# A gated two-branch spectral filter on one core: symmetric folds, a real-packed spectrum and quarter-size transforms in place of transposes

## The chip, the cores and the metric

The kernel runs on one NeuronCore of one Trainium2 chip. The metric is the device time of one execution in microseconds (us). "PE" is the matmul engine and "PEld" its weight loads, "DVE" the vector engine, "ACT" the scalar engine; "SPq" is the queue of the SyncE engine, which here only issues DMAs. Every number comes from a run or from its profile.

The times of the kernel before scatter: of its 11 runs beside one group of experiments, four took 301.8 to 305.1 us and seven 306.9 to 312.1; the latter are marked slow (over 1.5% above the fastest). By the same rule one of the four runs in the table below, that of 310.48 us, is slow, and so is the profiled execution, by its span of 309.5 us (in the runs listed the span is about 1.8 us below the time).

Ratios here are those of the fast runs of the same rounds, so not quite the ratios of the medians that I quote. Differences of about 1% between groups of runs should not be read.

## The reference

```python
def branch(x, w_r, w_i):                       # x: (1, 2048, 1024) bf16, w: (2048, 513)
    X = rfft2(x.astype(float32))               # over both axes
    return irfft2(X * (w_r + 1j * w_i), s=(2048, 1024)).astype(bfloat16)

g = sigmoid((x * gate_w).sum(-1, keepdims=True))
out = g * branch(x, A_w_r, A_w_i) + (1 - g) * branch(x, B_w_r, B_w_i)
```

The forward transform of x is shared. Each branch (A and B) multiplies the spectrum by its own weights W_A or W_B (4.2 MB each) and transforms back. Both kernels do this as small dense transforms by matmul: d (1024 columns) in one factor, the 2048 rows as 128 x 16.

## The kernel before

Each stage is a loop on PE; ACT and DVE evict PSUM between them (they copy the results of the matmuls, `PS` in the views, to the tiles of the next stage). The parts that matter here:

```python
# x is transposed by matmuls with IDENT, then the d transform: 16 x 8 x 3 matmuls of 342 columns
for n2 in range(16):
    for j in range(8):
        lhsT = AP(R_XT, j * 2048 + n2 * 128, ...)
        for ch in range(3):
            mm = e.matmul(bank(bset + ch, 0, ncols), lhsT, rhs, start=(j == 0), stop=(j == 7))      # L218
# ... 64 + 64 matmuls (L234, L240) ...
for g in range(16):                                    # 512 small transposes, L258
    for tt in range(8):
        for lh in range(4):
            mm = e.matmul(AP(PS, (32 * lh) * PSRS + ...), lhsT, IDENT[:], tile_position=(0, 32 * lh))
# ... K-point transform (L289/L290), then per branch the products on DVE and L312/L313 on PE,
#     inverse over n1 (L336), inverse over d: 16 x 2 x 8 matmuls of 512 columns (L360)

# the loads of W, in pieces of 128 elements (256 bytes); B's start when the d transform is over
@block.sync
def _(e):
    ...
    e.wait_ge(sem("pe_j1"), 16)
    w_dmas(e, 1, R_XT, "d_wB", (0, 2))
```

Of the kernel before, what the change touches and what calls it, by code (L numbers as in the profile page):

```python
# [4 lines left out]
dt = mybir.dt  # L5
ACT = mybir.ActivationFunctionType
ALU = mybir.AluOpType
AP = bass.AP

S, D, L = 2048, 1024, 513  # L10
NCOLX = 2 * 16 * L
NX = 128 * 128


def bf16_bits(a):
    a = np.ascontiguousarray(np.asarray(a, dtype=np.float32))
    u = a.view(np.uint32).astype(np.uint64)
    r = ((u + 0x7FFF + ((u >> 16) & 1)) >> 16).astype(np.uint16)
    return r


def make_consts():
    C = {}
    dd = np.arange(128)[:, None, None]
    j = np.arange(8)[None, :, None]
    l = np.arange(L)[None, None, :]
    ang = 2 * np.pi * ((128 * j + dd) * l % D) / D
    DF = np.concatenate([np.cos(ang), -np.sin(ang)], axis=2)
    C["DF"] = DF[:, 0:4, :].reshape(128, 4 * 2 * L)
    sg = (-1.0) ** np.arange(L)  # L30
    C["SGN"] = np.broadcast_to(np.concatenate([sg, sg])[None, :], (128, 2 * L)).copy()
    n1 = np.arange(128)[:, None, None]
    n2 = np.arange(16)[None, :, None]
    k1 = np.arange(128)[None, None, :]
    ph = -2 * np.pi * ((n1 * k1 * 16 + n2 * k1) % 2048) / 2048.0
    U2 = np.zeros((128, 16, 3, 128))
    U2[:, :, 0, :] = np.cos(ph)
    U2[:, :, 1, :] = np.sin(ph)
    U2[:, :, 2, :] = -np.sin(ph)
    C["U2"] = U2.reshape(128, 16 * 3 * 128)  # L40
    C["IDENT"] = np.eye(128)
    C["ONES"] = np.ones((128, 128))
    a16 = np.arange(16)
    th = 2 * np.pi * np.outer(a16, a16) / 16
    M16 = np.zeros((32, 32))
    M16[0:16, 0:16] = np.cos(th); M16[16:32, 0:16] = np.sin(th)
    M16[0:16, 16:32] = -np.sin(th); M16[16:32, 16:32] = np.cos(th)
    M16i = np.zeros((32, 32))
    M16i[0:16, 0:16] = np.cos(th); M16i[16:32, 0:16] = -np.sin(th)
    M16i[0:16, 16:32] = np.sin(th); M16i[16:32, 16:32] = np.cos(th)  # L50
    M16s = np.concatenate([M16[:, 16:32], M16[:, 0:16]], axis=1)
    M16iA = np.concatenate([M16i[0:16, :], -M16i[0:16, :]], axis=0)
    M16iB = np.concatenate([M16i[16:32, :], M16i[16:32, :]], axis=0)
    KF2 = np.zeros((128, 128)); KF2S = np.zeros((128, 128))
    KIA = np.zeros((128, 128)); KIB = np.zeros((128, 128))
    for lh in range(4):
        KF2[lh * 32:(lh + 1) * 32, lh * 32:(lh + 1) * 32] = M16
        KF2S[lh * 32:(lh + 1) * 32, lh * 32:(lh + 1) * 32] = M16s
        for r in range(32):
            for cc in range(32):  # L60
                KIA[lh * 32 + r, cc * 4 + lh] = M16iA[r, cc]
                KIB[lh * 32 + r, cc * 4 + lh] = M16iB[r, cc]
    C["KF2"] = KF2; C["KF2S"] = KF2S; C["KIA"] = KIA; C["KIB"] = KIB
    def pad128(m):
        o = np.zeros((128, m.shape[1])); o[0:m.shape[0]] = m
        return o
    C["M16PK"] = np.concatenate([pad128(M16), pad128(M16s), pad128(M16iA), pad128(M16iB)], axis=1)
    k1b = np.arange(128)[:, None, None]
    o2 = np.arange(16)[None, :, None]
    o1 = np.arange(128)[None, None, :]  # L70
    ph5 = 2 * np.pi * ((k1b * o1 * 16 + o2 * k1b) % 2048) / 2048.0
    U5 = np.zeros((128, 16, 4, 128))
    U5[:, :, 0, :] = np.cos(ph5) / S
    U5[:, :, 1, :] = np.sin(ph5) / S
    U5[:, :, 2, :] = -np.sin(ph5) / S
    U5[:, :, 3, :] = np.cos(ph5) / S
    C["U5"] = U5.reshape(128, 16 * 4 * 128)
    ll = np.arange(128)[:, None]
    dcol = np.arange(D)[None, :]
    Dinv = np.zeros((128, 8, D))  # L80
    for lh in range(4):
        lval = 128 * lh + ll
        cl = np.where(lval == 0, 1.0, 2.0) / D
        ang3 = 2 * np.pi * ((lval * dcol) % D) / D
        Dinv[:, lh * 2 + 0, :] = cl * np.cos(ang3)
        Dinv[:, lh * 2 + 1, :] = -cl * np.sin(ang3)
    C["DINV"] = Dinv.reshape(128, 8 * D)
    C["NSPAT"] = np.broadcast_to((((-1.0) ** np.arange(512)) / D)[None, :], (128, 512)).copy()
    one = np.zeros((128, 2)); one[:, 0] = 1.0
    C["ONE"] = one  # L90
    return C


def bass_gated_mix__spectral_gfnet__spectral_gfnet__prompt_kernel(
# [3 lines left out]
    cst = {k: nc.inline_tensor(bf16_bits(v), name=f"c_{k}") for k, v in C.items()}  # L98

    bfz = dt.bfloat16  # L100
    sb = lambda name, shape, dty=dt.bfloat16: nc.alloc_sbuf_tensor(name, shape, dty)
    R_XT = sb("R_XT", [128, 8 * 2048])
    R_L1 = sb("R_L1", [128, NCOLX])
    R_L2 = sb("R_L2", [128, NCOLX])
    R_C1 = sb("R_C1", [128, NCOLX])
    R_W = sb("R_W", [128, NCOLX])
    R_L4A = sb("R_L4A", [128, NCOLX])
    SGN = AP(R_L4A, 4096, [[NCOLX, 128], [1, 2 * L]])
    IDENT = sb("IDENT", [128, 128]); ONES = sb("ONES", [128, 128])
    KF2 = sb("KF2", [128, 128]); KF2S = sb("KF2S", [128, 128]); KIA = sb("KIA", [128, 128]); KIB = sb("KIB", [128, 128])  # L110
    M16PK = sb("M16PK", [128, 4 * 32])
    GWT = sb("GWT", [128, 8]); ONE2 = sb("ONE2", [128, 2])
    NSPAT = sb("NSPAT", [128, 512]); GROW = sb("GROW", [128, 2048])
    RBUF = sb("RBUF", [128, 2, 2, 2, 256])
    L3S = sb("L3S", [128, 128])
    XST = sb("XST", [128, 2, 128])
    WST = sb("WST", [128, 2, 128])
    PST = sb("PST", [128, 2, 128])
    G = sb("G", [128, 16], dt.float32); ZT = sb("ZT", [128, 16], dt.float32)
    PS = nc.alloc_psum_tensor("PS", [128, 4096], dt.float32)  # L120

    with nc.Block() as block:
        sems = {}
        info = {"n_c": 11}

        def sem(name):
            if name not in sems:
                sems[name] = nc.alloc_semaphore(name)
            return sems[name]

        rsX = 8 * 2048
        rs = NCOLX
        PSRS = 4096

        def bank(b, c0=0, n=512, p0=0, np_=128):
            return AP(PS, p0 * PSRS + b * 512 + c0, [[PSRS, np_], [1, n]])

        x2 = A_x[0]
        out2 = out[0]
        wsrc = {0: (A_w_r, A_w_i), 1: (B_w_r, B_w_i)}  # L140
        BN = "AB"

        def w_dmas(e, bb, region, semname, lhs):
            for c in range(2):
                for lh in lhs:
                    src = wsrc[bb][c][:, 128 * lh:128 * lh + 128].rearrange("(k2 k1) ll -> k2 k1 ll", k1=128)
                    dst = region[lh * 32 + c * 16: lh * 32 + c * 16 + 16, 0:NX].rearrange("p (k1 ll) -> p k1 ll", ll=128)
                    e.dma_start(dst, src).then_inc(sem(semname), 16)

        def wstar_dmas(e, bb, semname):  # L150
            for c in range(2):
                src = wsrc[bb][c][:, 512:513].rearrange("(k2 k1) o -> k2 (k1 o)", k1=128)
                with nc.allow_non_contiguous_dma(reason="N* W column gather (small)"):
                    e.dma_start(WST[c * 16:(c + 1) * 16, bb, :], src).then_inc(sem(semname), 16)

        @block.sync
        def _(e):
            e.dma_start(IDENT[:].bitcast(dt.uint16), cst["IDENT"].ap()).then_inc(sem("d_id"), 16)
            xv = x2.rearrange("(p r) d -> p r d", r=16)
            for h in range(2):  # L160
                e.dma_start(AP(R_L2, 8192 * h, [[rs, 128], [1024, 8], [1, 1024]]), xv[:, 8 * h:8 * h + 8, :]).then_inc(sem(f"d_x{h}"), 16)
            e.wait_ge(sem("pe_j1"), 1)
            w_dmas(e, 0, R_W, "d_wA", (0, 2))
            wstar_dmas(e, 0, "d_wA")
            e.wait_ge(sem("pe_j1"), 16)
            w_dmas(e, 1, R_XT, "d_wB", (0, 2))
            wstar_dmas(e, 1, "d_wB")
            e.wait_ge(sem("pe_j4"), 32)
            e.wait_ge(sem("pe_j4b"), 32)
            e.dma_start(R_L1[:, 8192:16384].bitcast(dt.uint16), cst["U5"].ap()).then_inc(sem("d_u5"), 16)  # L170
            e.wait_ge(sem("pe_i1sB"), 1)
            e.dma_start(R_L1[:, 0:8 * 1024].bitcast(dt.uint16), cst["DINV"].ap()).then_inc(sem("d_dinv"), 16)
            outv = out2.rearrange("(p r) d -> p r d", r=16)
# [12 lines left out]
        def wait_w(e, bb):  # L186
            e.wait_ge(sem("d_w" + BN[bb]), 16 * 6)
            e.wait_ge(sem("g_w" + BN[bb]), 16 * 4)

        @block.tensor  # L190
        def _(e):
# [30 lines left out]
            t = 0  # L222
# [364 lines left out]
```

## Time and profile before

| | before |
|---|---|
| median time | 306.91 us (4 runs, 305.11 to 310.48) |
| profiled span, instructions | 309.5 us, 5236 |
| PE / DVE / ACT busy | 239.5 / 133.9 / 119.0 us |
| d transform (L218) on the last chain | 56.9 us |
| inverse over d (L360) on the last chain | 17.8% of the span |

The first view is the page of the kernel before: span, busy time and share of each engine with its number of instructions, and three rows of 40 equal slices of the span (7.7 us each). A digit is the busy share in tenths; PEclk is the clock granted to PE in tenths.

```profile
span 309.5 us, 5236 instructions
PE 239.5 (77%) x2304; PEld 161.5 (52%) x2315; DVE 133.9 (43%) x234; ACT 119.0 (38%) x156; POOL 8.5 (3%) x12
...
PE   0464999999989640404289879799799989999995
...
PEclk9999999999999965555559979999999999999999
DMA  7942799999369999999100070000600001211121
```

After its first slices PE is busy nearly everywhere but in slices 14 to 20; from slice 15 on its clock is near half as well. The timeline of PE shows why: these are the transposes. Columns are start, duration, engine, line, operation and tiles, count, and in brackets the idle time before and what ended it.

```profile
104.99 1.63 PE L258 MATMUL PS<-IDENT,R_L 128*32 128x128 bf16 x77 [0.45 <-ACT L3S L405]
111.77 3.66 PE L258 MATMUL PS<-IDENT,R_L 128*32 128x128 bf16 x128 [5.15 <-issue]
125.91 3.67 PE L258 MATMUL PS<-IDENT,R_L 128*32 128x128 bf16 x128 [10.48 <-issue]
139.51 3.67 PE L258 MATMUL PS<-IDENT,R_L 128*32 128x128 bf16 x128 [9.93 <-issue]
151.46 1.65 PE L258 MATMUL PS<-IDENT,R_L 128*32 128x128 bf16 x51 [8.28 <-issue]
```

Four times PE stood 5 to 10 us waiting for nothing that the profile shows, the first time after 77 of these matmuls and then each time after 128, with as many weight loads. W_B's load in 256-byte pieces ran at that time (DMA digits at 9). These gaps are 33.8 us.

### The profile page before, as it was taken

The page shows a single profiled execution, that of the slowest core. Times are in us where ns is not written, and L with a number is a line of the kernel's source. Part 1 is how long each engine was busy: PE and PEld are TensorE (multiplying, and loading weights), DVE is VectorE, ACT ScalarE, POOL GpSimd, SP SyncE. Part 2 cuts the span into 40 slices and gives each one's busy share as a digit, 9 for nine tenths or more (in the row PEclk, how much of TensorE's full clock was granted, in tenths as well). Part 3 has the DMA queues.
Part 4 walks back from the last instruction along what each step waited for, and adds up shares of the span by engine and source line. Part 5 has one row for each costly group of instructions (what it writes and reads, how often), then busy time and mean ns, then how long its engine had stood idle before and what let it go on. Part 6 is the DMA issues. An engine that isn't in the chain of part 4 may idle for free.

```text
span 309.5 us, 5236 instructions
## 1 busy us (share of the span) xinstructions
PE 239.5 (77%) x2304; PEld 161.5 (52%) x2315; DVE 133.9 (43%) x234; ACT 119.0 (38%) x156; POOL 8.5 (3%) x12
## 2 busy tenths in 40 slices
PE   0464999999989640404289879799799989999995
PEld 0463666666645440404122278798799954444442
DVE  0338000000037820303139999999555513434343
ACT  0083222233266420202159959899665520000000
POOL 0000500000050000000000000000000000000000
PEclk9999999999999965555559979999999999999999
DMA  7942799999369999999100070000600001211121
GB/s 259 394 107 89 169 103 102 100 100 87 3 55 75 74 78 78 83 80 29 2 0 0 2 271 2 0 2 3 235 40 0 2 2 69 101 68 70 68 102 68
DMA packets 31973, 24.56 MB, mean 79 GB/s; under 512 B 27472, under 2 KB 27600, under 8 KB 31312
## 3 DMA queue, kind: packets, MB, share of 16 engines
q1 hardware_dynamic: 27792, 16.83, 34.0%
q0 software_dynamic: 1152, 4.19, 16.0%
q10 hardware_dynamic: 3008, 3.22, 3.3%
q8 instruction: 18, 0.29, 0.6%
q14 instruction: 3, 0.02, 0.1%
HBM read 20.04 MB, written 4.19 MB: 78 GB/s over the span
## 4 chain that ended last, share of the span: by engine, by line
PE 60%; ACT 14%; issue 12%; DVE 7%; ACTq 5%; another core or an unknown queue 0%
PE PS L218 18%; PE PS L360 18%; PE PS L336 9%; ACT R_W L437 6%; ACT R_L4A L437 6%; PE PS L258 5%; PE PS L234 5%; DVE R_L L499 4%; ACTq L374 4%; PE PS L202 2%; PE PS L289 1%; PE PS L290 1%; PE PS L312 1%; DVE R_C L463 1%; ACT R_XT L384 1%
## 5 line engine op out<-in xcount | busy, mean ns | idle before, releaser
L218 PE MATMUL PS<-R_C,R_XT 128*128 128x342 bf16 (+1 forms) x384 | 56.9, 309 | 1.7 <-issue 1.7
L360 PE MATMUL PS<-R_L 128*128 128x512 bf16 x250 | 54.9, 379 | 1.7 <-ACT R_L L449 1.4
L218 PEld LDWEIGHTS PS<-R_C,R_XT 128*128 128x128 bf16 x384 | 37.4, 98 | 21.0 <-issue 1.8
L360 PEld LDWEIGHTS PS<-R_L 128*128 128x128 bf16 x256 | 25.0, 98 | 31.2 <-issue 1.2
L258 PE MATMUL PS<-IDENT,R_L 128*32 128x128 bf16 x512 | 14.3, 301 | 34.3 <-issue 33.8
L554 DVE SCALAR_TENSOR_TENSOR R_C<-NSPAT,ZT,PS 128x512 bf16<-128x512 bf16 x32 | 23.9, 747 | 36.0 <-PE PS L360 36.0
L312 PE MATMUL PS<-KIA,R_L 128*128 128x128 bf16 x256 | 35.1, 231 | 4.7 <-DVE R_L L523 2.5
L479 DVE CAST R_L<-PS 128x512 bf16<-128x512 f32 x16 | 11.1, 693 | 63.0 <-PE PS L234 63.0
L312 PEld LDWEIGHTS PS<-KIA,R_L 128*128 128x128 bf16 x256 | 32.2, 146 | 7.4 <-issue 4.7
L313 PE MATMUL PS<-KIB,R_L 128*128 128x128 bf16 x256 | 34.5, 228 | 0.0
L313 PEld LDWEIGHTS PS<-KIB,R_L 128*128 128x128 bf16 x256 | 32.6, 147 | 0.0
L391 ACT ACTIVATE R_L<-PS 128x1026 bf16<-128x1026 f32 x16 | 16.4, 1026 | 41.9 <-PE PS L218 41.9
L258 PEld LDWEIGHTS PS<-IDENT,R_L 128*32 128x32 bf16 x512 | 13.2, 163 | 35.2 <-issue 35.2
L493 DVE CAST R_L<-PS 128x1024 bf16<-128x1024 f32 x8 | 9.8, 1223 | 37.9 <-PE PS L258 37.9
L336 PE MATMUL PS<-RBUF,R_L4A 128*128 128x256 bf16 x128 | 24.4, 272 | 1.5 <-ACT R_W L440 1.5
L202 PE MATMUL PS<-IDENT,R_L 128*128 128x128 bf16 x128 | 11.4, 270 | 17.0 <-DMA R_L<-in_A_x_dram 10.6
L336 PE MATMUL PS<-RBUF,R_W 128*128 128x256 bf16 x128 | 24.4, 272 | 0.0
L411 ACT ACTIVATE R_L<-PS 128x1024 bf16<-128x1024 f32 x8 | 8.2, 1027 | 40.3 <-PE PS L258 40.3
L449 ACT ACTIVATE R_L<-PS 128x512 bf16<-128x512 f32 x32 | 17.4, 594 | 13.6 <-PE PS L336 13.6
L499 DVE CAST R_L<-PS 128x1024 bf16<-128x1024 f32 x16 | 18.4, 1214 | 5.5 <-PE PS L289 5.5
L202 PEld LDWEIGHTS PS<-IDENT,R_L 128*128 128x128 bf16 x128 | 10.6, 126 | 17.5 <-issue 10.6
L437 ACT ACTIVATE R_L4A<-PS 128x1024 bf16<-128x1024 f32 x16 | 18.4, 1272 | 3.6 <-PE PS L313 3.5
(60 smaller groups left out, 250.8 us busy)
## 6 DMA issues: line engine op xcount, KB each, us to landing
R_L<-in_A_x_dram SPq DMA_DIRECT2D x2, 2048.0 KB, 12.1
out_dram<-R_C SPq DMA_DIRECT2D x16, 256.0 KB, 2.0
R_L<-c_U SPq DMA_DIRECT2D x1, 2048.0 KB, 7.6
R_L<-c_DINV SPq DMA_DIRECT2D x1, 2048.0 KB, 7.7
R_C<-c_U ACTq DMA_DIRECT2D x1, 1536.0 KB, 6.1
R_C<-c_DF ACTq DMA_DIRECT2D x1, 1026.0 KB, 16.3
R_W<-in_A_w_r_dram SPq DMA_DIRECT2D x2, 512.0 KB, 21.7
R_W<-in_A_w_r_dram POOLq DMA_DIRECT2D x2, 512.0 KB, 16.1
```

What stands on the lines that cost most here:

```text
L202: mm = e.matmul(AP(PS, bb0 * 512 + (n2 - 8 * h) * 128, [[PSRS, 128], [1, 128]]), lhsT, IDENT[:], start=True, stop=True)
L218: mm = e.matmul(bank(bset + ch, 0, ncols), lhsT, rhs, start=(j == 0), stop=(j == 7))
L258: mm = e.matmul(AP(PS, (32 * lh) * PSRS + b0 * 512 + tt * 128, [[PSRS, 32], [1, 128]]), lhsT, IDENT[:], start=True, stop=True, tile_positi ...
L312: e.matmul(o_ap, lhsA, KIA[:], start=True, stop=False)
L313: mm = e.matmul(o_ap, lhsB, KIB[:], start=False, stop=True)
L336: mm = e.matmul(o_ap, lhsT, RBUF[:, slot, bb, cp, :], start=(i == 0), stop=(i == 3))
L360: mm = e.matmul(bank(b, 0, 512), lhsT, rhs, start=(i == 0), stop=(i == 7))
L391: e.activation(dst, src, ACT.Copy).then_inc(sem("a_j1"), 1)
L437: e.activation(dst, src, ACT.Copy).then_inc(sem("a_i1" + BN[bb]), 1)
L449: ins = e.activation(dst, src, ACT.Copy)
L499: e.tensor_copy(dst, src).then_inc(sem("v_j4x"), 1)
L554: e.scalar_tensor_tensor(out=dst, in0=NSPAT[:, 0:512], scalar=ZT[:, o2:o2 + 1], in1=bank(b, 0, 512), op0=ALU.mult, op1=ALU.add).then_inc(s ...
```

## The change

The new kernel computes the same thing by another factorization. x is folded on DVE (sums and differences of the halves, then of one half with the reversed other half), so that each transform over d is a quarter of the size. The 128-point spectrum of the real input is stored packed as 64 real pairs. Every matmul leaves its result in the layout that the next one needs, so no transposes are left. The gate is computed from the transformed data. Of the 513 columns of the spectrum the last, l=512, has a way of its own: a small product (`p512`), a few small matmuls (`v512`), and 16 small DMAs per branch (`v512_row`) that bring it to partition 0, where it forms one row. The stages are named in the code: `d` is the transform over d, `s2` the 16-point transform after it, `i1` the first inverse transform, and the inverse d stage follows.

All instructions go through a small tracker: `S.op(engine, instruction, reads, writes)` orders an operation behind the last writer of each key that it reads, and behind the last writer and the readers of each key that it writes.

```diff
-            for n2 in range(16):                       # before: dense d transform, transposes ...
-                for j in range(8):
-                    for ch in range(3):
-                        mm = e.matmul(bank(bset + ch, 0, ncols), lhsT, rhs, ...)
...
+    def op(self, eng, fns, reads=(), writes=(), dma=False):
+        ...
+        for k in writes:
+            o.deps |= self.writer.get(k, set())
+            o.deps |= self.readers.get(k, set())
...
+    def wload(b, kgs):                                 # W in rows of 513 elements (1026 bytes)
+        for kg in kgs:                                 # 16 groups
+            prs = []
+            for c in range(2):                         # real, imaginary: 2 DMAs of 64 rows each
+                ...
+            dma("sp", prs, [], [("W", b, kg)] + (["zrow", "gwt"] if b else []))
...
+    for n2 in range(0, 16, 2):                         # A: fold, 128-point transform, gate rows
+        fold(2, R1, n2 * 1024, RING, ...)
+        ...
+    for t in range(16 + 5):                            # B
+        if t < 16:
+            stage_d(t)
+        if 1 <= t < 17:
+            stage_s2(t - 1)
+        if t >= 5:
+            stage_i1(0, t - 5)
+        if t >= 2 and t % 2 == 0:
+            prod(t // 18, t // 2 - 1 - t // 18 * 8)
+        if t == 3:
+            wload(1, range(16))
+            cload("sp", DI, "DI", 2048)
+            cload("sp", RM, "RM", 2048)
+        if t == 17:
+            x512()
+            p512(0)
+            p512(1)
+        if t == 19:
+            v512(0)
+            v512(1)
+    v512_row(0)                                        # 16 DMAs of 128 elements on SPq
...
+    for t in range(16 + LAG):                          # C: i1 of B, inverse d of A
+        ...
+    for t in range(17):                                # D: inverse d of B, last stage, unfold, output
+        ...
```

## The prediction

> **What bounds the kernel now.** The page gives PE 239.5 us busy (77% of 309.5 us), DVE 133.9 (43%), ACT 119.0 (38%); the chain that ended last is 60% PE and 12% "issue". It is a row of stages, nearly each with another limit: forward d transform (384 matmuls of 342 columns, 56.9 us in the chain), its 64+64 matmuls, 512 transposing matmuls, two evictor-bound stages (DVE L499, ACT L437: 1.27 us per 1024 columns), inverse (55 us). The waits view charges 33.8 us to "issue" before the transposes (L258): four gaps of 5 to 10 us, each after 128 matmuls + 128 weight loads, while small-packet W loads fill the DMA (share above 1, packets under 512 B). I read these as instruction supply held up by those loads. PEclk falls to 0.5 there; the Trainium skill ("TensorE: Matmul & The Clock Gate", Part 1) describes this half clock after idle windows, and the trace agrees (0.50 from 120 to 145 us).
>
> **What the change does.** Folds use the symmetry of cos/sin, so matmul columns fall to about 246,000: stage 1 16k, d 33k, s2 33k, i1 66k, inverse d 66k, last 33k; at the traced 0.215 us per 512 columns that is about 103 us. PE instructions halve, the 512+128 transposes and their gaps go, W comes as 1026-byte rows. Evictions become 128 tiles of 1024 columns (traced: ACT 1.02, DVE 1.22 us), most on ACT: about 125 us. DVE gets folds (32 of 1024 elements, 0.68 us as L522 shows), full complex products (16 x (2 x 1.22 + 2 x 0.68) = 61 us) and unfolds (64 x 0.42): about 110 us plus some evictions. PE stops being the bound; ACT and DVE share it. bf16 two-input DVE at two elements per cycle is what "VectorE: DVE Perf Modes" (The perf-mode tier table) says, and L522's 679 ns per 1024 agrees; no trace shows it yet for the reversed reads and writes.
>
> **Sum by stage (estimates from those durations).**
> A, folds + stage 1: x lands about 4.5 us, DVE 8 x 2.7 us + gate 1.5, tail 2: 30 us (PE cold, not binding).
> B, d, s2, products, i1 of A: 48 evictions, 42 on ACT at 1.03, DVE 10 products 38 us + 6 evictions; ramps: 53 us.
> C, i1 of B, inverse d of A: 31 ACT evictions + 4 sigmoids + table load 36 us, plus a stall of about 5 us: the l=512 row goes by 16 tiny DMAs (0.45 us issue each, 2 us landing) and only some four tiles of i1 cover them.
> D, inverse d of B, last stage: DVE 64 x 0.42 + evictions = 33 us, same stall 5, tail 3: 41 us.
> Total 165 us. All removed PE time and gaps are on the old chain, so nearly all of the difference counts.
>
> **Right if:** ACT and DVE each about 115 to 135 us busy, PE about 110 to 140; no "issue" gaps over 5 us before PE; two PE gaps of about 5 us before the first inverse-d matmul of A and of B, released by the row DMAs; reversed folds 0.68 us; chain mostly ACT and DVE.
>
> **Wrong if:** reversed DVE operands run at one element per cycle (+9 us in A, +4 in D); 140 small W DMAs on one queue arrive late (products wait for DMA; the l=512 product of B waits for all of W_B and blocks DVE); fixed engine assignment makes ACT and DVE wait on each other beyond my 5 to 10%; PE drops to half clock in B to D, where it would bind.
>
> Predicted 165 us, range 150 to 185; faster by over 2% 0.98, within 2% 0.01, slower 0.01.

## The result, and the profile after

| | before | after |
|---|---|---|
| median time | 306.91 us | 218.76 us (4 runs, 218.39 to 220.41) |
| ratio of fast runs | | 0.7136 (95%: 0.7089 to 0.7184) |
| span, instructions | 309.5 us, 5236 | 217.0 us, 2645 |
| PE / DVE / ACT busy | 239.5 / 133.9 / 119.0 | 129.6 / 120.3 / 120.6 us |

The ratio is the mean time of the changed kernel's fast runs over that of the other's fast runs of the same rounds. The change is clearly faster, but by 88 us and not by the 142 forecast; 218.8 lies far outside the range of 150 to 185. The page of the changed kernel, the same rows (a slice is now 5.4 us):

```profile
span 217.0 us, 2645 instructions
PE 129.6 (60%) x999; PEld 91.4 (42%) x1008; DVE 120.3 (55%) x193; ACT 120.6 (56%) x130; POOL 0.2 (0%) x4
...
PE   0368777999999960000000284499799029998970
...
PEclk9999999999999985555555558799999856999996
DMA  6999344343112221222222510000000000233243
```

The busy times are those of the forecast. The loss is idle time: slices 16 to 22 are empty on PE, and slice 32. The view of waits names the first hole, in total us, times, and the longest:

```profile
DVE P L310 <- DMA R<-in_B_w_i_dram: 43.0, 1, 43.0
PE PS L307 <- DVE P L310: 42.2, 1, 42.2
ACT V L296 <- PE PS L307: 42.1, 1, 42.1
...
PE PS L307 <- DMA R<-V: 9.3, 1, 9.3
```

One DVE instruction, the l=512 product of B (its output is P), waits 43 us for a load of W_B; PE and ACT wait behind it, from about 81 to 123 us. The timeline of the SyncE queue shows how W was issued. First W_A, two issues to a line, then W_B:

```profile
46.45 1.23 SPq L313 DMA_DIRECT2D R<-in_A_w_r_dram  x2
47.73 1.23 SPq L313 DMA_DIRECT2D R<-in_A_w_i_dram  x2
49.00 1.23 SPq L313 DMA_DIRECT2D R<-in_A_w_r_dram  x2
...
90.05 1.17 SPq L313 DMA_DIRECT2D R<-in_B_w_r_dram  x2
91.26 1.23 SPq L313 DMA_DIRECT2D R<-in_B_w_i_dram  x2
94.12 1.17 SPq L313 DMA_DIRECT2D R<-in_B_w_r_dram  x2
95.34 1.23 SPq L313 DMA_DIRECT2D R<-in_B_w_i_dram  x2
98.28 1.17 SPq L313 DMA_DIRECT2D R<-in_B_w_r_dram  x2
...
121.24 0.58 SPq L313 DMA_DIRECT2D DI<-c_DI  x1
...
127.06 49.36 SPq L313 DMA_DIRECT2D R<-V  x32
```

W_A's issues follow each other: four issues, one group, every 2.55 us. W_B's groups are 4.1 us apart, with a pause after every four. The waits of the SyncE queue itself name what ended the pauses, 15 times for 16 groups:

```profile
SPq L313 <- DMA R<-in_B_w_i_dram: 24.6, 15, 1.7
```

The chain that ended last has the pauses as well: it alternates between issues of 0.59 us and landings of W_B of about 2.2 us. The code gives the reason. Each of the 16 loads of W_B *writes* the keys "zrow" and "gwt", because its memory held the gate rows before. Only the first load has to wait for their readers. But to the tracker each load is also the last writer of these keys for the next load, so it makes every load wait until the one before has landed: a write-after-write order between loads to different addresses.

So there are three things on one queue: W_A takes from 5.4 to 51.9 us to issue (70 DMAs), W_B then takes until 121 us, and behind it stand the constant DI of the inverse d stage and the 16 row DMAs.

### The profile page after: what moved, and what is told of

The parts are those of the page before. It is cut to its first block, busy times and chain, and to the rows that moved or that the text cites. A ratio compares the mean times of both kernels' runs of the same rounds, so it can differ in the third digit from the quotient of the medians.

```text
span 217.0 us, 2645 instructions
## 1 busy us (share of the span) xinstructions
PE 129.6 (60%) x999; PEld 91.4 (42%) x1008; DVE 120.3 (55%) x193; ACT 120.6 (56%) x130; POOL 0.2 (0%) x4
## 4 chain that ended last, share of the span: by engine, by line
ACT 24%; DMA 20%; SPq 19%; DVE 17%; PE 12%; issue 7%; DVEq 0%
SPq L313 19%; DMA R<-in_B_w_i_dram 17%; ACT R L296 13%; PE PS L307 12%; DVE RING L310 9%; ACT RING L296 9%; DVE R L310 5%; DMA R<-in_A_x_dram 2%; DVE RING L298 2%; ACT GROW L551 1%; DMA R<-V 1%; ACT L551 1%; DVE P L310 0%; DVEq L209 0%
## 5 line engine op out<-in xcount | busy, mean ns | idle before, releaser
L296 ACT ACTIVATE R<-PS 128x1024 bf16<-128x1024 f32 (+1 forms) x80 | 76.1, 1035 | 27.2 <-PE PS L307 27.2
L310 DVE TENSOR_TENSOR RING<-R 128x2048 bf16<-128x2048 bf16 (+1 forms) x48 | 48.0, 1040 | 14.2 <-ACT R L296 8.4
L296 ACT ACTIVATE RING<-PS 128x1024 bf16<-128x1024 f32 x40 | 43.0, 1133 | 19.6 <-PE PS L307 19.6
L310 DVE TENSOR_TENSOR RING<-RING 128x512 bf16<-128x512 bf16 (+1 forms) x96 | 44.5, 508 | 7.4 <-PE PS L307 4.1
L307 PE MATMUL PS<-DI,R 128*128 128x256 bf16 x256 | 35.3, 286 | 16.6 <-DMA R<-V 9.3
L307 PE MATMUL PS<-KI,RING 128*128 128x256 bf16 x256 | 36.6, 294 | 5.2 <-DVE RING L310 3.2
L307 PEld LDWEIGHTS PS<-DI,R 128*128 128x128 bf16 x256 | 25.4, 102 | 25.4 <-issue 15.8
L307 PEld LDWEIGHTS PS<-KI,RING 128*128 128x128 bf16 x256 | 25.2, 105 | 13.2 <-DVE RING L310 4.0
L307 PE MATMUL PS<-DM,R 128*128 128x256 bf16 x128 | 16.5, 273 | 0.3 <-ACT RING L296 0.2
L307 PE MATMUL PS<-RING,S 128*128 128x1 bf16 (+2 forms) x91 | 15.8, 304 | 1.3 <-ACT RING L296 1.1
L307 PEld LDWEIGHTS PS<-DM,R 128*128 128x128 bf16 x128 | 11.8, 98 | 3.0 <-ACT RING L296 1.1
```

What stands on the lines that cost most here:

```text
L296: S.op("act", lambda e: e.activation(outap, inap, ACT.Copy), reads, writes)
L307: return lambda e: e.matmul(o, l, r, start=start, stop=stop, skip_group_check=True)
L310: return lambda e: e.tensor_tensor(out=o, in0=a, in1=b, op=op)
```

## The experiments

Theory: the compute is as summed, and the excess comes from the SyncE queue: the false order of W_B's loads, then what stands behind them on the queue, then the issue time of the row DMAs. The first rival: bandwidth of the DMA or the memory limits W_B. The second: what matters is the place of the l=512 product of B, which blocks DVE in order. Every experiment gave a correct result. The changed kernel itself was not run again, so the distance of an experiment from its 218.76 us lies between chips.

| run | median us | ratio to before (95%) |
|---|---|---|
| the change | 218.76 | 0.7136 (0.7089 to 0.7184) |
| e1_tokens | 196.07 | 0.6379 (0.6302 to 0.6457) |
| e2_move | 215.33 | 0.7030 (0.6956 to 0.7104) |
| e3_both | 191.80 | 0.6253 (0.6192 to 0.6314) |
| e6_row_by_PE | 201.81 | 0.6579 (0.6521 to 0.6638) |
| e12_few_issues_alone | 178.01 | 0.5834 (0.5770 to 0.5898) |
| e4_all_three | 159.12 | 0.5228 (0.5201 to 0.5256) |
| e5_fewer_W_issues | 158.67 | 0.5219 (0.5191 to 0.5246) |
| e8_four_slots | 158.89 | 0.5225 (0.5195 to 0.5255) |
| e9_last_stage_on_ACT | 157.68 | 0.5170 (0.5129 to 0.5212) |
| e10_gate_later | 156.92 | 0.5143 (0.5098 to 0.5187) |
| e11_both_small | 155.59 | 0.5104 (0.5064 to 0.5145) |
| b1_before_W_later | 300.53 | 0.9878 (0.9793 to 0.9963) |

### e1_tokens: only the false order goes

```diff
-            dma("sp", prs, [], [("W", b, kg)] + (["zrow", "gwt"] if b else []))
+            dma("sp", prs, [], [("W", b, kg)] + (["zrow", "gwt"] if b and kg == 0 else []))
```

The loads are still issued by one queue in order, so all stand behind the wait of the first.

> Only the false order between W_B's loads is removed: the marks zrow and gwt are put on the first load group alone. Theory (each group of W_B waits for the group before it to land, 4.1 us a group in place of the 2.5 us that its four issues take): W_B is issued from 52 to about 95 us, the l=512 product of B starts at about 98 us and not 122.9, the PE gap before it falls from 42 us to about 17, time about 193 us. Rival (DMA or HBM bandwidth limits W_B): groups still take about 4 us each and the time stays within 3 us of 218.8.

Measured 196.07 us, 22.7 us less. A line of the waits view of this run, then the end of W_B in its SyncE timeline:

```profile
DVE P L310 <- DMA R<-in_B_w_i_dram: 19.9, 1, 19.9
```

```profile
96.38 1.23 SPq L313 DMA_DIRECT2D R<-in_B_w_r_dram  x2
97.65 1.23 SPq L313 DMA_DIRECT2D R<-in_B_w_i_dram  x2
98.92 0.58 SPq L313 DMA_DIRECT2D DI<-c_DI  x1
```

W_B now comes at the pace of W_A and the wait falls from 43.0 to 19.9 us. The bandwidth rival is out: with the marks (the keys "zrow" and "gwt") taken off 15 of the 16 loads the same bytes were issued in 46 us (52.8 to 98.9) and not 69. In the stretch of the hole (81 to 123 us) the DMA engines of the changed kernel were busy only 26%.

### e2_move and e3_both: the place of the product

```diff
         if t == 17:
             x512()
             p512(0)
-            p512(1)
         if t == 19:
             v512(0)
-            v512(1)
...                                                    # in the loop of stage C
+        if t == 12:
+            p512(1)
+        if t == 13:
+            v512(1)
```

In e2 the false order stays, in e3 it is removed as in e1.

> Only the l=512 product of B and its matmuls are moved behind all other products in the queues; the false order stays. Rival (the place of this product, which blocks DVE in order, is the whole cause): the 42 us gap goes and the time falls by 35 us or more, to about 183 us. Theory (the SP queue is the cause: the 16 row DMAs and the DI constant stand behind W_B on it, so the first inverse-d matmul of A waits for them anyway): the gap moves to that matmul, which starts at about 134 us in place of 138.3; time about 214 us.

> Both edits. Theory: W_B is through at about 97 us, the row DMAs of A run from 97 to 109, first inverse-d matmul of A at about 109 us, time about 190 us, only some 4 us better than the tokens alone. Rival (the place of the product matters for itself): 20 us or more better than the tokens alone, about 170 us.

Measured 215.33 us for e2 and 191.80 for e3: the move is worth 3.4 us alone (between chips) and 4.3 us once the false order is gone (e3 against e1, on one chip). The 43 us wait at the product is gone in e2, and another wait has taken its place. The waits of e2, then of e3:

```profile
PE PS L307 <- DMA R<-V: 53.7, 2, 44.4
```

```profile
PE PS L307 <- DMA R<-V: 30.4, 2, 21.2
```

R<-V are the row DMAs. They stand behind W_B on the queue, and the first inverse-d matmul of A needs them: it started at 133.4 us in e2 and at 110.0 in e3 (138.3 in the changed kernel). So the profile's longest wait named a true waiter, but taking it away gave 3.4 us of its 43. The rival "the product's place is the cause" falls, as a sufficient cause.

### e6_row_by_PE: the row without DMAs

```diff
-        dma("sp", [(ap(VR[b], 2048 + 8 * k, [[128, 16], [1, 8]], 0, 1), ap(V5, b * 128, ..., k, 1))
-                   for k in range(16)], ...)
+        for half in range(2):                          # replaces v512 as well
+            s = slot()
+            for j in range(8):
+                k = 8 * half + j
+                for c in range(2):                     # one output row: partition 0
+                    fns.append(mm(pslot(s, j * 128, [[1, 128]], 0, 1), ap(P5, o + 16 * c + k, [[1, 1]]),
+                                  ap(KI, (0 if k else 512) + c * 256 + 128, [[1, 128]]), c == 0, c == 1))
+            S.op("pe", fns, ...)
+            ev(1024, ap(VR[b], 2048 + 64 * half, [[8, 8], [128, 16], [1, 8]], 0, 1), ...)
```

(A single DMA for the row, tried first, did not build: too many dimensions.) The false order of W_B is left in.

> Only the l=512 row is changed: 32 one-row matmuls and two evictions per input write it at partition 0, in place of 16 small DMAs; W_B's loads are left as they are. Theory (16 issues of 0.63 us and 1.7 us of landing make 11.8 us before each inverse-d stage): the gaps of 5.6 us before the first inverse-d matmul of A and of about 11 us before that of B fall to under 3 us each, about 12 us less, 206 us. Rival (the gap of 5.6 us is instruction supply, as its releaser 'issue' says): the first gap stays, about 8 us less, 211 us.

Measured 201.81 us, 17.0 us less, more than either side expected. The two PE gaps of the changed kernel, from its timeline:

```profile
138.34 1.86 PE L307 MATMUL PS<-DI,R 128*128 128x256 bf16 x8 [5.57 <-issue]
...
177.69 2.72 PE L307 MATMUL PS<-DI,R 128*128 128x256 bf16 x12 [9.26 <-DMA R<-V]
```

The same two places in e6, the first inverse-d matmuls of A and of B:

```profile
133.50 1.04 PE L307 MATMUL PS<-DI,R 128*128 128x256 bf16 x8
...
160.26 5.58 PE L307 MATMUL PS<-DI,R 128*128 128x256 bf16 x48
```

No idle time is left before either. The first gap was labelled "issue", yet it went with the row DMAs; its label was not its cause. From the first inverse-d matmul to the end of the span the changed kernel takes 78.7 us and e6 67.0. One row costs 16 issues, 0.63 us apart, and 1.7 us of landing: 11.8 us, where I had put 9.2.

### e12_few_issues_alone: coarser loads

A W input is loaded by 34 DMAs of 16 partitions x 8 rows, in two groups, in place of 70 DMAs in sixteen groups. The place of the product and the row DMAs stay as they are. The marks do not: the edit keeps "zrow" and "gwt" on the first of the two groups only, so the false order between loads is gone here, as in e1. The expectation below overlooked that.

```diff
-        for kg in kgs:                                 # 16 groups; per half: 64 partitions x 1 row
+        for k0 in range(0, 16, 8):                     # 2 groups; every 4th partition x 8 rows
...
+                def one(p0, kg, nk, r0, dk):
+                    return (AP(T, p0 * P + kg * 2 * NS + c * NS, [[4 * P, 16], [2 * NS, nk], [1, n]]),
+                            AP(src.tensor, src.offset + r0 * n, [[128 * n, 16], [dk * n, nk], [1, n]]))
...
-            dma("sp", prs, [], [("W", b, kg)] + (["zrow", "gwt"] if b else []))
+            dma("sp", prs, [], [("W", b, kg) for kg in range(k0, k0 + 8)] + (["zrow", "gwt"] if b and k0 == 0 else []))
```

> The changed kernel with only W's loads coarser (34 DMAs of 128 rows per input in two groups, not 70 of 64 rows in sixteen); order of the product, row DMAs and the marks stay, so that the false order holds back one group and not fifteen. Theory: W_B is issued by about 59 us, the wait of 42 us at the l=512 product goes, the row DMAs are issued from about 82 us, first inverse-d matmul of A at about 94 us, then 78.7 us to the end as before: span 173, time about 174 us. Rival (coarse DMAs move bytes too slowly, or W_A comes too late): 180 us or more.

Measured 178.01 us, 4 more than expected. W_B was issued from 34 to 58 us and nothing waited for it any more. Its second group (16 DMAs) followed the first without a pause:

```profile
41.30 5.74 SPq L313 DMA_DIRECT2D R<-in_B_w_i_dram  x9
47.09 5.09 SPq L313 DMA_DIRECT2D R<-in_B_w_r_dram  x8
```

The first inverse-d matmul of A came at 96.6 us instead of 94, because the last i1 of A was evicted only at 85 and the row DMAs started then; from there it took 78.8 us to the end, as in the changed kernel. So the run stands beside e1, which has the order off and 70 DMAs: half the DMAs for the same bytes take 24 us to issue in place of 46, and the time falls by another 18 us (178.01 against 196.07, on different chips). That points to the number of issues, and not the bytes, as what paced W_B in e1; with W_B in time the early place of the product costs nothing. Whether coarser loads would hide the false order too is not shown: no run has the one without the other.

### e4_all_three and e5_fewer_W_issues: is the compute as summed?

e4 is e3 with the row by PE, and with DI and RM loaded before W_B:

```diff
         if t == 3:
-            wload(1, range(16))
             cload("sp", DI, "DI", 2048)
             cload("sp", RM, "RM", 2048)
+            wload(1, range(16))
```

e4 thus has four edits, in spite of its name; the order of DI, RM and W_B was not tried alone. e5 is e4 with the coarse loads of e12.

> Tokens off, product of B moved, row written by PE, and the two constants DI and RM loaded before W_B. Theory (the excess over the predicted 165 us is these queue effects and no compute): the first inverse-d matmul of A starts at about 89 us (110.0 with tokens and move alone), no PE gap over 5 us between 36 us and the end, time about 157 us, at or below the predicted 165. Rival (stages C and D are slower in themselves than summed, or products now wait for W_B, which is issued until about 97 us): 170 us or more.

> As the run before it in this call, with W loaded by 34 DMAs of 16 partitions x 8 rows per input in place of 70 of 64 rows: the same bytes and rows, half the issues, W_B issued by about 57 us and not 97. Theory (once the false order and the queue effects are gone, W_B is in time although its issue is slow): same time within 2 us. Rival (W_B's arrival still paces the products of B): 5 us or more faster.

Measured 159.12 us for e4 and 158.67 for e5. By the medians, which are of different chips, the queue effects together are worth 59.6 us (0.7136 to 0.5228 by the ratios), more than the sum of the three single edits (22.7 + 3.4 + 17.0 = 43.1; the reordering of DI and RM is not among these): each alone leaves another of them in the way. e5 shows that W's issue is no longer on the path. The table of stretches, first the changed kernel (columns: length, busy us of PE, PEld, DVE, ACT and POOL with counts, granted clock, DMA share, GB/s):

```profile
0.00:34.00 34.00, 19.32 (x179) 12.81 (x179) 21.47 (x36) 19.03 (x22) 0.20 (x4) 1.00 0.73 238
34.00:81.00 47.00, 43.20 (x354) 30.77 (x356) 36.19 (x43) 41.17 (x42) 0.00 (x0) 0.99 0.29 73
81.00:123.00 42.00, 0.39 (x4) 0.10 (x1) 0.13 (x1) 1.08 (x2) 0.00 (x0) 0.50 0.26 67
123.00:138.00 15.00, 8.22 (x44) 5.30 (x44) 15.00 (x21) 5.28 (x6) 0.00 (x0) 0.72 0.17 61
138.00:167.00 29.00, 26.42 (x229) 22.10 (x230) 16.55 (x24) 26.15 (x30) 0.00 (x0) 0.94 0.00 1
167.00:178.00 11.00, 1.74 (x15) 1.19 (x14) 1.23 (x1) 2.16 (x3) 0.00 (x0) 0.74 0.02 0
178.00:217.00 39.00, 30.31 (x188) 19.15 (x190) 29.72 (x69) 25.70 (x27) 0.00 (x0) 0.89 0.29 109
```

And e4:

```profile
0.00:36.00 36.00, 22.55 (x192) 14.42 (x193) 21.65 (x37) 18.59 (x22) 0.20 (x4) 1.00 0.72 228
36.00:81.00 45.00, 41.81 (x335) 29.36 (x334) 36.16 (x43) 41.07 (x41) 0.00 (x0) 1.00 0.44 110
81.00:89.00 8.00, 7.75 (x71) 6.31 (x70) 8.00 (x10) 5.86 (x6) 0.00 (x0) 0.79 0.45 106
89.00:119.00 30.00, 27.18 (x264) 22.96 (x262) 24.57 (x36) 29.11 (x33) 0.00 (x0) 1.00 0.18 43
119.00:157.00 38.00, 30.70 (x211) 19.97 (x209) 31.07 (x70) 27.96 (x30) 0.00 (x0) 0.99 0.30 111
```

Up to 81 us the two are alike. Then the changed kernel loses 42 us in the hole, some 7 us after it (15 us for what e4 does in 8: PE stood 5.6 us of it before the row, and the clock, 0.50 in the hole, was still 0.72 on average) and the 11 us hole before stage D. The last stage is the same to 1 us.

### e8, e9, e10, e11: what is left

Four small edits on e4. e8: `nslots[0] = 4` before stage D, so that its PSUM tiles rotate over four slots and not three. e9: `eng="act"` on the evictions of stage D, so that all 32 are on ACT. e10: the last gate row and the small instructions after it move behind the first d stages (and use PSUM bank 7). e11: e9 and e10.

```diff
+    nslots[0] = 4                                      # e8, ahead of stage D
...
-            ev(1024, ap(RING, VBO + n2 % 2 * 1024, ...), pslot(s, ...), ..., [("VB", n2 % 2)] + ...)
+            ev(1024, ap(RING, VBO + n2 % 2 * 1024, ...), pslot(s, ...), ..., [("VB", n2 % 2)] + ..., eng="act")   # e9
-        ev(1024, ap(RING, o, [[1, 1024]]), pslot(s, 0, [[1, 1024]]), [("ps", s)], [("o", r)])
+        ev(1024, ap(RING, o, [[1, 1024]]), pslot(s, 0, [[1, 1024]]), [("ps", s)], [("o", r)], eng="act")          # e9
...
-    gate_row(3)                                        # e10: out of stage A ...
...
+        if t == 1:                                     # ... into the loop of stage B
+            gate_row(3, 7)
+        if t == 3:
+            ...                                        # the 16 small matmuls and the DVE product
```

> As the first of this call, with a fourth PSUM slot (the two spare banks) in the last stage. Theory (three slots and fixed ACT/DVE order make the engines wait on each other there: about 38 us of stage for 30 us of work on PE and on DVE): 2 to 4 us faster. Rival (DVE work and the dependences of the last stage set it): within 1 us.

> As e4_all_three, with all 32 evictions of the last stage on ACT (8 were on DVE). Theory (PE waits there on DVE evictions that stand behind twelve unfold instructions in DVE's order, 4.8 us in all): 2 to 3 us faster, about 157. Rival (ACT then binds, 32 x 1.0 us): within 1 us or slower.

> As e4_all_three, with the last gate row, its 16 small matmuls and their DVE product moved behind the first two d stages. Theory (PE stands about 3.5 us in this chain, matmul, eviction of one partition, matmul, before the first d matmul): 3 us faster, about 156. Rival (it delays W_B, or the same work is only moved): within 1 us.

> Both small edits on e4_all_three: 5 us faster if they are independent, about 154 us; the candidate for the best version.

e8 missed: 158.89 us, nothing gained. More slots do not help where the slot is not what the engines wait for. e9, e10 and e11 ran on another chip than e4, so I compare ratios to the kernel before. e9's interval overlaps with that of e4: a gain of about 1 us may be there, but it is not shown. e10 is a gain of some 2 us (0.5143 against 0.5228; the first d matmul came at 31.2 us, and at 35.2 in e4). e11 is clearly below e4: at 155.59 us it is the best version, half the time of the kernel before. It is 3.5 us below e4 by the medians (of different chips), where 5 were expected of the two edits together.

### b1_before_W_later: the gaps of the kernel before

```diff
-            e.wait_ge(sem("pe_j1"), 16)                # on the SyncE queue and on the POOL queue
+            e.wait_ge(sem("pe_j3"), 16)
             w_dmas(e, 1, R_XT, "d_wB", (0, 2))
```

> The kernel before, with the load of W_B started after the transposes and not before them. Theory (four 'issue' gaps, 33.8 us, are instruction supply held up by W_B's small packets): gaps go, about 273 us against 308. Rival (the gaps belong to the 512 transposes themselves): time within 5 us of before.

Measured 300.53 us: by fast runs 1.2%, about 4 us, and not the 35 expected. (Against the median of before it is 7 us, but most runs behind that median were slow.) The timeline of PE at the transposes, then a line of the waits:

```profile
107.12 4.08 PE L258 MATMUL PS<-IDENT,R_L 128*32 128x128 bf16 x205 [0.45 <-ACT L3S L405]
111.57 2.36 PE L258 MATMUL PS<-IDENT,R_L 128*32 128x128 bf16 x128 [0.36 <-issue]
115.29 2.44 PE L258 MATMUL PS<-IDENT,R_L 128*32 128x128 bf16 x128 [1.37 <-issue]
119.02 1.19 PE L258 MATMUL PS<-IDENT,R_L 128*32 128x128 bf16 x51 [1.29 <-issue]
```

```profile
DVE R_L L522 <- DMA WST<-in_B_w_i_dram: 19.1, 1, 19.1
```

The gaps fell from 33.8 us to about 3, at the same boundaries of 128 matmuls: W_B's load made them long. The transposes end at 120 us and not at 153. So the rival's number came (within 5 us of before), but not its mechanism: the transposes run without these gaps. The kernel gained far less than the 31 us because W_B now lands at 187 us and its first product waits 19.1 us for it: it starts at 187.7 us, and at 197.7 in the profile of before. W_B's load costs this kernel time in either place. That the short remaining gaps are instruction supply fits their regular spacing, but no run shows it directly.

## Why the prediction was wrong

- **The bound before: right.** PE and the gaps before the transposes. That W_B's load makes those gaps long is shown by b1; "instruction supply" stays an inference.
- **Busy times after: right.** I said ACT and DVE 115 to 135 us each and PE 110 to 140; measured 120.6, 120.3 and 129.6.
- **The other signs: in part.** The chain was not mostly ACT and DVE (24% and 17%): the SyncE queue and its DMAs had 39%. Before A's first inverse-d matmul came the gap of about 5 us (5.57), but labelled "issue"; before B's it was 9.26 us.
- **Reversed folds: right.** 688 ns for 1024 elements with one reversed input, 682 without. The Trainium skill ("Vector Engine (DVE) Microarchitecture Reference", 5.1) lists how the engine streams an operand with a negative step as not measured; this trace shows its time, without a loss.
- **Stage A, 30 us: 4 us short.** The first d matmul came at 34.2. The chain of the last gate row, matmul to one-partition eviction to matmul, was not in the sum; e10 takes most of it away.
- **Stage B, 53 us: a little long.** It was 47 us up to 81 us, where only the last of A's i1 was missing.
- **Stage C, 41 us including a stall of 5: this is the step that failed.** It took 97 us, from 81 to 178. The sum charged W_B nothing. I had named the danger ("the l=512 product of B waits for all of W_B and blocks DVE") and gave it no cost, because I took the loads to stream. I had read the tracker's rule and the load's keys in the diff and not put them together: with "zrow" and "gwt" written by all 16 loads they run one at a time, 4.1 us a group in place of 2.55. In place of the free load there was a hole of 42 us. e1 shows that the order alone is worth 22.7 us; the wait of 19.9 us that is left in e1 is the issue of 70 DMAs for each W, and it is gone in e12 with half as many. In e4 the same stage takes 38 us (81 to 119).
- **The issue of small DMAs was mis-sized.** I used 0.45 us; measured 0.63 us from issue to issue. 70 of them put W_A's end at 51.9 us and so W_B's start, and 16 of them made the row 11.8 us and not 9.2; of these PE stood idle 5.6 us for A and 9.3 us for B, where I had put 5 each. I also saw the queue as the path of the loads only, and not as the path of DI and of the row behind them; e2 shows that this is what keeps the time up when the product is moved.
- **Stage D, 41 us including a stall of 5: near, in part by luck.** It took 39 us from 178 to 217, but the stall, the hole of 11 us, fell before it: the work itself was 3 us longer than the 36 summed.
- **The clock.** I named the half clock as a risk. It came as a consequence of the holes: 0.50 from 81 to 123 us, as "TensorE: Matmul & The Clock Gate" (Part 1) of the Trainium skill describes for idle windows. It is not a cause of its own: with the holes gone (e4) the clock is 0.986 over the run.
- **The total.** With the queue effects edited away (e4, the row by PE) the kernel runs in 159.12 us, within the range forecast; the forecast without its two stalls of 5 us would have been 155. The sum of the compute held to about 4 us; what it lacked was one ordered queue.

## What to carry to other kernels

Count DMAs per queue and give each its issue time, then walk the queue in order as you would walk an engine: a constant or a tiny copy behind a long load is as late as the load. When a tracker takes "writes" as order, ask of each key who wrote it last; a key put on a whole family of loads to guard the first makes them run one after another. And when the profile names one long wait, ask what comes next on the same queue before you move the waiter: here moving it gave back 3.4 of 43 us, mending the queue (with the row taken off it) 59.6.

## What the Trainium skill lacked or had wrong

- "DMA: Bandwidth & Descriptors" (Issuing engines are not separate DMA queues) says that the sequencer's time to initiate a DMA "is usually small relative to the DMA itself". Not so here: a DMA of 64 KB took 0.63 us of the queue from issue to issue and about 2.2 us to land, and in e1 the 70 of W_B held the queue for 46 us (52.8 to 98.9) while the DMA engines were busy 35%. The page has the sequencer's time per DMA only in cycles, for "previous generations", in a table about trn3. What SyncE took here from issue to issue was 0.63 us for the row's DMAs of 256 bytes as well as for 64 KB, and 0.48 to 0.54 us for four constants of 4 to 512 KB (3.40 to 5.43 us in the changed kernel).
- "Vector Engine (DVE) Microarchitecture Reference" (5.1) names steps of 1 and -1 alike for the mode of two results per cycle, but has how the engine streams a negative step under "Not measured": a two-input bf16 operation on 1024 elements with one input at step -1 took 688 ns, with none 682 ns.
- I found no page that says that bulk loads in small pieces can make gaps before PE: four gaps, 33.8 us in all, beside 256-byte loads, and about 3 us with those loads moved away (b1). If the gaps are instruction supply, which no run shows directly, it belongs to "Runtime: NRT & Kernel Launch" (Instruction fetch mechanics).
- Nothing was found wrong in "TensorE: Matmul & The Clock Gate" (Part 1): 0.50 in the hole of 42 us, 0.99 to 1.00 in the long stretches where PE was kept busy. It also fell once without a long hole: in e4 PE was busy about a third of the time from 78 to 81 us, and the clock was 0.50 from 82 to 84 us; in e5 and e8 it stayed at 1.00 around there, which no run explains.
